# A new stored order and engine choice for the same pieces of an attention and spatial-gating kernel

## The chip, the core and the metric

The kernel runs on one core of a Trainium2 chip. TensorE multiplies matrices; VectorE, ScalarE and GpSimd do elementwise work; SyncE's queue issues the loads and stores. The metric is the time of one execution in microseconds of the device, as the median of several runs.

## What is computed

The inputs q, k and v have 8 batches, 8 heads, 576 positions and 64 channels. For each batch and head two attentions are added: one over means of four neighbouring positions (144 of them), repeated four times, and one where a position sees only those less than 4 away. The heads side by side are x (8, 576, 512), which goes through a gated block:

```python
    out_d = sm_attn(q_d, k_d, v_d)              # q_d, k_d, v_d: means over 4 positions
    out_up = np.repeat(out_d, factor, axis=2)
    mask = np.abs(pos[:, None] - pos[None, :]) < factor
    scores = np.where(mask, scale * np.matmul(q, k.transpose(0, 1, 3, 2)), -1000000000.0)
    ...
    return out_up + out_local
...
    h = x @ w_in                                # then gelu (tanh form)
    u, v = (h[..., :d_ff // 2], h[..., d_ff // 2:])
    v_n = (v - mu) / np.sqrt(var + 1e-06) * g_ln
    v_s = np.einsum('ts,bsd->btd', w_sg, v_n) + b_sg[None, :, None]
    return x + (u * v_s) @ w_out
```

## The kernel before, in words

The work is cut into 2105 small pieces ("tasks"), each with a name and one function that issues its instructions. A table in the source, `ORDER`, lists all names in the order in which they are issued; `/V`, `/A`, `/P` or `/S` behind a name chooses the engine (VectorE, ScalarE, GpSimd, SyncE's queue) where a piece can go to more than one. `place` walks the table once and deals out the buffers: 8 PSUM banks ("ps"), 10 wide buffers ("X") and 38 others ("R"). Each engine then works through its own pieces strictly in the table's order; a piece waits for what it reads and for its buffer to come free.

```python
    for word in ORDER.split():
        name, _, e = word.partition("/")
        t = named.pop(name)
        for k in t.takes:
            where[k] = free[k[0]].pop(0)
        ...
        order.append((t, e or next(iter(t.engines))))
```

Attention pieces carry the number g of a pair of heads, 0 to 31 (four pairs a batch). `lq`, `lk`, `lv`, `lw` load Q, K, V for the pooled part and V for the local part. `qs` and `ks` sum four neighbouring positions of Q and K (one reduction on VectorE, line 391, or two additions on GpSimd, lines 394 and 395). `Y` are the pooled scores (line 445), `S` the local ones (line 424, for the first four pairs with a mask product, line 417); from pair 4 on `YS` does both. `ma`, `mb` add the mask, `mx`, `my` take row maxima, `nx`, `ny` make the bias, `ea`, `eb`, `ec` the exponentials, `re`, `rc` the reciprocal of the sums, `np`, `nq` normalize (lines 506 and 509). `T`, `U`, `t` are the turns: transposes of the probabilities on TensorE (lines 512 and 521), which `pa`, `pb`, `pc`, `pe` copy out of PSUM. `D` multiplies the probabilities with V (lines 573 and 589), `vs` having summed V for it on GpSimd. `oe`, `od`, `xa`, `xb` put the two attentions together as x. `xh` and `xl` split x into a high and a low part (line 608 is the low part), `xc` copies a corner of it.

Y, S, YS and D are the 64-row products: each instruction uses 64 (or 48) rows and 64 columns of TensorE's array, four of them side by side. The turns and all products below use more than 64 rows; they are called 128-row here.

The gated block has per batch b: `v` (line 691, for batch 0 cut into `vk` and `v`), its gelu `vg`, statistics `vb`, root `vp`, normalization `vn` and split `vh`, `vl`; `u` (line 769) with gelu `ua`; `s` (line 769), the product over positions, with `sa` and gate `sm`; the split of the gated values `gh`, `gl`; and `o` (line 769) with the addition `oa` and the store `os`. The `w...` pieces load the weights and split them into two parts on ScalarE, VectorE and GpSimd. `wq0` to `wq4` are the loads of the spatial weights, `whq` and `wlq` their split.

TensorE issues one instruction after the other. No loop remains at run time: the table alone sets which product stands next to which.

Of the kernel before, what the change touches and what calls it, by code (L numbers as in the profile page):

```python
# [93 lines left out]
my3 ny4/V wuy2 eb3 wq4 lq5 qs5/V pc1/V mx4 lv1/S lk5 ny3/A t1 pe1/A wlq0/P np2/P T2 pa2/A ec3 re3/A wbz2 wuz3 rc3 wbz1
nq2/P U2 wty0 t2 wty2 pb2/A wuz1 wuz2 pc2/A pe2/V ks5/V ec4 lw1/S D1 oe1/V np3/P YS5 T3 od1 xa1 wqz3/A why0/A nx4/V
xb1 wly0/V vk3.0 wtz2 nq3/P U3 xh1/V xl1/P lv2 whq4/A lw2 wtz1 ea4 pa3/A vk2.0 ma5 eb4 lv3 my5 ny5/A re4/A mb5 wbz3
lk6 ks6/P pb3/A pc3/A wlq4/V rc4 np4/P D2 oe2/V od2 xa2 wr1 wqr1/A vk0.0 t3 lq6 ec5 wr2 why2/A wqr2/A wtz3 pe3/A mx5
nx5/A lw6 xb2 xh2/A vk3.1 whz1/A vk2.1 vk0.1 wbr1 lw3 whz2/A wz0 wqz0/A wuz0 wr0 vk4.0 T4 pa4/V xc1 wly2/P vk1.0 wbr2
vk4.1 vk1.1 D3 xl2/P xc2 vk4.2 vk2.2 vk1.2 whz3/A wbz0 oe3/A nq4/P U4 eb5 ea5 vk0.2 od3 xa3 xb3 vk3.2 wlz3/V wq1
whq1/A xh3/V t4 wtz0 lk12 xl3/V xc3 v0.1 pb4/A wlq3/V lq7 wlz1/V qs7/V qs6/V wlz2/P vg0.1 vb0.1 lv4 vs4 re5/V v0.2  # L100
v0.3 v0.0 pc4/A vg0.0 vb0.0 v0.4 lk9 whz0/A va0.4/A pe4/A vp0.0 u0.6 wq2 lq9 whq2/V vj0.4 vp0.1 rc5 nq5/P np5/P ua0.6
vg0.3 vg0.4 wur1 wr3 wqr3/A lw4 lq8 YS6 my6 ma6 u0.4 ua0.4 vn0.1 vh0.1/A vb0.4 ny6/A vg0.2 u0.7 vn0.0 vh0.0/A vp0.4
u0.5 ec6 mb6 vb0.2 wur3 vb0.3 mx6 wur0 wur2 ua0.5 U5 lk7 wlz0/P ks7/V nx6/A vn0.4 vh0.4/A wtr1 b lv5 vs5 ua0.7 lw11
lk8 ks8/V u0.2 ua0.2 wbr3 wlq2/V T5 pa5/A u0.0 ua0.0 vl0.1/V u0.1 vp0.2 vn0.2 vh0.2/A u0.3 ua0.3 vl0.0/V vp0.3 vn0.3
wlq1/V pb5/A ua0.1 vl0.2/V vh0.3/A vl0.3/P YS7 ma7 whr1/A wlr1/P ea6 D4 oe4/V qs9/V vl0.4/V my7 s0.1 sa0.1 sm0.1/P
pc5/V od4 xa4 s0.0 wtr3 eb6 sa0.0 mb7 qs8/V wtr2 re6/A rc6 t5 pe5/A ny7/A s0.3 sa0.3 ec7 mx7 whr3/A nx7/A YS8 my8 xb4
ma8 mb8 np6/P ks9/V wqr0/A nq6/P lk11 lv6 lq10 lw5 D5 oe5/A mx8 eb7 ny8/A ea7 T6 pa6/V sm0.0/V gh0.0/A s0.2 sa0.2
qs10/P od5 xa5 U6 s0.5 sm0.3/P sa0.5 lw8 vs6 wlr3/V sm0.2/P gh0.1/A re7/A s0.7 t6 s0.4 lv11 gl0.0/P xb5 pb6/V pc6/A
pe6/A wbr0 rc7 sm0.5/P lk14 xh5/A whr2/A lk10 sa0.7 np7/P lk15 ec8 lw7 lw14 lv7 sa0.4 nx8/V s0.6 sm0.4/P sa0.6 gh0.2/A
sm0.6/V gl0.2/V YS9 lq12 gl0.1/V D6 oe6/V ma9 mb9 mx9 nx9/V T7 sm0.7/P gh0.3/A lv12 lq11 gl0.3/P o0.6 oa0.6 ea8 eb8  # L110
re8/A od6 xa6 o0.4 oa0.4 my9 nq7/P U7 rc8 pa7/A pb7/V pc7/V nq8/V o0.7 ks10/V wtr0 ny9/A whr0/A t7 ec9 xb6 xh6/A pe7/V
o0.5 oa0.5 os0.2 YS10 oa0.7 os0.3 vs7 wlr0/P D7 oe7/A eb9 xh4/V ea9 re9/A ma10 mb10 mx10 od7 ks12/V wlr2/P t8 o0.3
np8/P T8 xa7 xb7 xh7/V o0.2 oa0.2 lq14 xl4/P xl5/V rc9 np9/V o0.0 lv9 lq13 xl6/P xc6 lv8 vs8 xc4 lq15 U8 pa8/A pb8/A
# [15 lines left out]
o1.2 oa1.2 re15/A pc14/A pe14/A vs13 D13 oe13/A od13 D14 my16 ny16/V u2.4 vb2.1 vp2.1 vp2.2 nx16/A eb16 rc15 np15/V
ec16 vn2.1 vb2.0 o1.3 ua2.4 o1.7 oa1.7 T15 o1.4 oa1.4 ea16 re16/A rc16 nq15/P o1.0 vp2.0 vn2.0 vh2.0/V vn2.2 xa13  # L130
oa1.0 vg2.4 vb2.4 pa15/A oe14/A u2.5 ua2.5 vh2.1/A vh2.2/A vp2.4 o1.5 oa1.5 vb2.3 u2.6 ua2.6 od14 o1.1 oa1.1 oa1.3
ks17/V t15 xb13 lv15 vn2.4 u2.0 vp2.3 vl2.1/P np16/P os1.0 lk18 xh12/A xa14 xl12/V vs15 U15 u2.7 T16 pa16/V xb14 u2.2
pb15/A pc15/A pe15/V vh2.4/V vl2.4/V u2.1 vl2.0/V ua2.0 ua2.2 ua2.1 YS17 ma17 vl2.2/V vn2.3 vh2.3/A mb17 ua2.7 xh13/V
my17 ny17/A ec17 lw15 D15 nq16/V oe15/A u2.3 od15 xa15 xb15 ks18/V vl2.3/P s2.1 sa2.1 sm2.1/P xh15/A xl15/V s2.7 s2.0
xl13/P YS18 ma18 xc15 ks20/P ua2.3 mb18 mx17 nx17/V mx18 nx18/A lk19 s2.2 ea17 sa2.0 xh14/V xl14/V U16 s2.3 sa2.3 t16
sm2.0/V gh2.0/A s2.5 sm2.3/V sa2.5 sa2.2 sm2.2/P lv20 eb17 re17/A pb16/A ea18 s2.4 sa2.4 gh2.1/A sm2.5/V rc17 pc16/A
s2.6 my18 ny18/A ec18 nq17/V eb18 np17/V re18/A sm2.4/P lw16 sa2.6 lv17 sa2.7 gl2.1/V u3.0 v3.1 xc13 U17 vs17 xc14
v3.2 vg3.2 vg3.1 sm2.6/V sm2.7/P gh2.3/A t17 rc18 pe16/V ks19/P xc12 v3.3 vg3.3 qs19/P gl2.0/P YS19 ua3.0 T17 pa17/V
# [850 lines left out]
```

## Time and profile before

| | |
|---|---|
| median of 3 runs | 582.2 us (581.97 to 583.54) |
| profiled execution | 582.29 us, its span 580.5 us |
| granted clock of TensorE over the span | 0.997 |
| instructions | 17400, of them 6992 matmuls and as many weight loads |
| moved | 52.64 MB read from HBM, 9.44 MB written |

The span runs from the first to the last instruction of the program; the execution's time is 1.8 us longer. Busy times are unions of an engine's instructions. TensorE's matmuls overlap each other, so what a matmul costs in a row of them is read from the distance of their starts, not from its own duration. "Idle before" is the time in which an engine did nothing just ahead of an instruction, and the arrow names what ended it; "issue" there means that nothing in the profile did.

### The profile page before, as it was taken

Reading aid. Unit: us, or ns where it says so; the run is one execution under the profiler, and the core shown is the slowest. Engines: PE = TensorE matmul, PEld = TensorE weight load, DVE = VectorE, ACT = ScalarE, POOL = GpSimd, SP = SyncE. Lnnn points to the kernel's source line nnn. Section 1 sums busy time; section 2 is a strip of 40 time slices with the busy share of each in tenths; the row PEclk is TensorE's granted clock in tenths of the full one; section 3 lists DMA queues with packets and bytes.
Section 4 is the critical chain, followed back from the end, with each engine's and each line's share of the span. In section 5 each row is a group of like instructions: output and inputs, shape, how many; then the busy total and the mean of one; then the engine's idle time right before and its main releaser. Section 6 shows DMA issues by size and latency. Waiting matters only on the chain.

```text
span 580.5 us, 17400 instructions
## 1 busy us (share of the span) xinstructions
PE 555.8 (96%) x6992; PEld 518.5 (89%) x6992; DVE 423.9 (73%) x926; ACT 350.5 (60%) x1237; POOL 312.1 (54%) x388
## 2 busy tenths in 40 slices
PE   5679999999999999999999999999998999999997
PEld 4568999889998899989999899989998899998997
DVE  5998899988988567848578778885967655653663
ACT  4988896759788864755438497728756357311200
POOL 4777857855378433574454646561475646541030
PEclk9999999999999999999999999999999999999999
DMA  8999256342132014161213606221255001010004
GB/s 312 350 284 336 83 151 191 124 142 69 57 106 76 23 44 129 53 201 49 70 38 103 213 25 190 78 84 65 76 164 140 22 1 57 1 43 1 21 0 184
DMA packets 30608, 63.20 MB, mean 109 GB/s; under 512 B 3520, under 2 KB 3776, under 8 KB 30528
## 3 DMA queue, kind: packets, MB, share of 16 engines
q1 hardware_dynamic: 30384, 61.79, 33.4%
...
q10 hardware_dynamic: 144, 0.30, 0.2%
q14 instruction: 25, 0.20, 0.1%
HBM read 52.64 MB, written 9.44 MB: 107 GB/s over the span
## 4 chain that ended last, share of the span: by engine, by line
PE 82%; DVE 9%; POOL 3%; issue 3%; ACT 2%; DMA 1%; DVEq 0%; ACTq 0%; POOLq 0%
PE ps L769 50%; PE ps L691 17%; PE ps L445 3%; PE ps L512 2%; PE ps L521 2%; PE ps L424 2%; PE ps L589 2%; PE ps L573 2%; POOL R L826 1%; POOL R L814 1%; DMA R<-in_qT_dram 1%; DVE R L221 1%; DVE R L596 1%; DVE X L432 1%; DVE R L740 1%
## 5 line engine op out<-in xcount | busy, mean ns | idle before, releaser
L769 PE MATMUL ps<-wsg_h,R 128*128 128x288 f32 x576 | 122.9, 300 | 1.2 <-DVE R L760 0.7
L769 PE MATMUL ps<-R,weight_r 128*128 128x288 f32 x768 | 110.0, 298 | 1.4 <-DVE R L826 0.6
L769 PE MATMUL ps<-X,weight_z 128*128 128x288 f32 x512 | 110.9, 299 | 0.0
L769 PEld LDWEIGHTS ps<-R,weight_r 128*128 128x128 f32 x768 | 103.4, 188 | 2.9 <-DVE R L826 0.9
L691 PE MATMUL ps<-weight_y,X 128*128 128x512 f32 x320 | 99.2, 402 | 0.3 <-DVE weight_y L326 0.2
L769 PEld LDWEIGHTS ps<-wsg_h,R 128*128 128x128 f32 x576 | 93.7, 188 | 2.0 <-DVE R L760 0.9
L484 ACT ACTIVATE X<-X,nb 128x64 f32<-128x64 f32 x280 | 93.5, 337 | 3.1 <-DVE nb L463 2.8
L769 PE MATMUL ps<-wsg_l,R 128*128 128x288 f32 x320 | 92.7, 295 | 0.0
L769 PEld LDWEIGHTS ps<-X,weight_z 128*128 128x128 f32 x512 | 84.5, 188 | 0.7
L769 PE MATMUL ps<-R,weight_z 128*128 128x288 f32 x256 | 75.4, 295 | 0.0
L691 PEld LDWEIGHTS ps<-weight_y,X 128*128 128x128 f32 x320 | 57.4, 188 | 12.0 <-DVE weight_y L326 0.5
L732 POOL TENSOR_TENSOR rs<-rs,nhalf 128x1 f32<-128x1 f32 (+1 forms) x40 | 23.3, 587 | 82.6 <-DVE rs L723 76.7
L769 PEld LDWEIGHTS ps<-wsg_l,R 128*128 128x128 f32 x320 | 60.3, 188 | 0.0
L807 DVE SCALAR_TENSOR_TENSOR vs<-ps,small_sb,b_sb 128x288 f32<-128x288 f32 x64 | 32.3, 512 | 29.1 <-PE ps L769 26.8
L484 ACT ACTIVATION_READ_ACCUMULATOR X<-X,nb 128x1 f32 x280 | 53.1, 189 | 0.0
L814 POOL TENSOR_TENSOR R<-R,vs 128x288 f32<-128x288 f32 x30 | 27.8, 929 | 44.5 <-DVE vs L807 43.3
L221 ACT COPY R<-ps 112x288 f32<-112x288 f32 (+4 forms) x75 | 27.8, 391 | 38.6 <-PE ps L521 16.2
L691 PE MATMUL ps<-weight_y,R 128*128 128x512 f32 x128 | 50.5, 394 | 0.6 <-issue 0.6
L788 ACT ACTIVATE R<-ps 128x288 f32<-128x288 f32 x64 | 24.8, 411 | 40.8 <-PE ps L769 34.9
L408 POOL TENSOR_TENSOR pairs<-R 112x256 f32<-112x256 f32 x56 | 46.7, 834 | 3.6 <-DMA R<-in_v_dram 3.5
L769 PEld LDWEIGHTS ps<-R,weight_z 128*128 128x128 f32 x256 | 48.2, 188 | 0.2
L721 DVE BATCH_NORM_STATS2 st<-R 128x6 f32<-128x512 f32 (+1 forms) x40 | 27.4, 686 | 27.5 <-ACT R L703 25.8
...
## 6 DMA issues: line engine op xcount, KB each, us to landing
...
```

The lines of the kernel that those rows point to most:

```text
L221: (nc.scalar.copy if e == "A" else ENG[e].tensor_copy)(**kw)
L408: ENG[e].tensor_tensor(out=pairs, in0=v[:, 0:2], in1=v[:, 2:4], op=ALU.add)
L424: nc.tensor.matmul(out=sp[i][os, c * KB:(c + 1) * KB], lhsT=q[hs, t * QB:t * QB + KB], rhs=k[hs, t * QB:t * QB + KB], start=not early, sto ...
L445: nc.tensor.matmul(out=st["sdv"][n][os, cs], lhsT=qd2[par][hs, i * QC:i * QC + HD], rhs=st["kd"][hs, ks], start=True, stop=True)
L484: nc.scalar.activation(out=st["ms"][:, t, :], in_=src, func=AF.Exp, bias=st["nb"][:, t:t + 1], scale=scale, accum_out=sums[par][:, t:t + 1])
L691: nc.tensor.matmul(out=acc, lhsT=r32(l), rhs=r32(weights[f"y{k}"][:, 0, w]), start=(i == 0 and ks[0] == 0), stop=(i == len(ops) - 1 and ks ...
L721: nc.vector.bn_stats(out=st6[0:n], in_=v[0:n])
L732: nc.gpsimd.tensor_tensor(out=rs[0:n], in0=rs[0:n], in1=nhalf[0:n], op=ALU.pow)
L769: nc.tensor.matmul(out=acc[:, 0:HALF], lhsT=r32(l), rhs=r32(r), start=(first and n == 0), stop=(last and n == len(ops) - 1))
L788: nc.scalar.activation(out=us[i // 2][:, half(i)], in_=at["ps", "m", b, "u", i][:, 0:HALF], func=AF.Gelu_apprx_tanh)
L807: nc.vector.scalar_tensor_tensor(out=vsb[i], in0=at["ps", "m", b, "s", i][:, 0:HALF], scalar=g_sb[:, i // 2:i // 2 + 1], in1=b_sb[:, half( ...
L814: ENG[e].tensor_tensor(out=u[:, half(i)], in0=u[:, half(i)], in1=vsb[i], op=ALU.mult)
```

## The change

Only `ORDER` differs: the same 2105 names stand in it in another order, some with another engine. No piece, no size and no buffer count is changed. Of the pieces with a choice of engine, VectorE has 14 fewer, GpSimd 15 more and ScalarE one fewer; among them GpSimd takes 24 normalizations `np` where it had 19 and 24 of the `vl` where it had 18, ScalarE takes 22 of the `xh` where it had 13 and 20 of the `pe` where it had 13, and gives up 9 of 19 `oe` and 9 of 26 `re`. On the queues of loads the first K comes by ScalarE's queue and the first Q by SyncE's, the other way round than before.

The table's rows tell a reader little; one of each:

```diff
-nq0/P U0 lq4 mx2 nx2/A wly3/V pa0/V pb0/V pc0/V lv0/S t0 eb1 pe0/A whq0/V wty1 why1/V wly1/P lk3 ks3/V lq3 S3 re1/A
...
+wqy3/V nq0/V T0 why0/V wly0/P t0 U0 pa0/V pb0/V pc0/V pe0/V Y2 my2 wqz1/V nx2/A eb1 re1/V why1/V rc1 np1/P nq1/P lk4
```

What that does to an engine shows in the engine's own rows (line, operation, what it writes and reads, size). The first place is GpSimd's queue in the opening. Names: `half`, `qd` and `kd` are the sums of Q and K, `pd` and X (line 506) the normalized probabilities, `weight_y` the weights of v, line 319 and line 326 two steps of their split, line 608 the low part of x. Before, from the second step of weight y1 on:

```order
L326 TENSOR_TENSOR weight_y1_332<-R5_198,weight_y1_332 128x512
L394 TENSOR_TENSOR half_380<-R9_303 128x288
L395 TENSOR_TENSOR qd0_75<-half_380 128x144
L506 TENSOR_TENSOR X1_241<-X1_241,rc1_95 128x640
L608 TENSOR_TENSOR R18_463<-R17_457,X4_461 128x576
L394 TENSOR_TENSOR half_475<-R16_385 128x288
L395 TENSOR_TENSOR kd0_83<-half_475 128x144
L509 TENSOR_TENSOR pd1_88<-pd1_88,rc1_95 128x9x48
```

and now, from the same step on:

```order
L326 TENSOR_TENSOR weight_y1_339<-R3_147,weight_y1_339 128x512
L394 TENSOR_TENSOR half_449<-R13_356 128x288
L395 TENSOR_TENSOR qd0_75<-half_449 128x144
L394 TENSOR_TENSOR half_463<-R19_438 128x288
L395 TENSOR_TENSOR kd1_84<-half_463 128x144
L319 TENSOR_TENSOR R14_359<-R14_359,weight_z1_235 128x512
L608 TENSOR_TENSOR R27_600<-R18_434,X5_503 128x576
```

The sum `kd0` that YS4 reads stood behind the low part of x (L608); it has moved to VectorE, `kd1` here is pair 3's, and the low part of x stands behind the sums and a weight's step.

The second place is TensorE at pair 19. `X` read in line 512 and `pd` in line 521 are its probabilities; lines 769 are products of s and u, line 424 is the end of YS21. Before, its turn T, then a product of u, and later U and t apart from it:

```order
L769 MATMUL ps_4852<-wsg_h,R_4699 128x288
L769 MATMUL ps_4852<-wsg_l,R_4699 128x288
L512 MATMUL ps_4868<-small_sb,X_4314 128x122 x4
L769 MATMUL ps_4877<-X_3707,weight_z_902 128x288
L769 MATMUL ps_4877<-R_3711,weight_z_902 128x288
```

and now T, t and U in one row behind the 64-row products of YS21:

```order
L424 MATMUL ps_4943<-R_3956,R_3688 64x64 x2
L424 MATMUL ps_4944<-R_3956,R_3688 64x64 x2
L512 MATMUL ps_4965<-small_sb,X_4266 128x122 x4
L521 MATMUL ps_4970<-small_sb,pd_88 112x112 x2
L512 MATMUL ps_4981<-small_sb,X_4266 128x122
L521 MATMUL ps_4981<-small_sb,pd_88 112x112 x3
L769 MATMUL ps_4989<-wsg_h,R_4489 128x288
```

The turn left its place between two 128-row products and came to stand between 64-row products and a 128-row one; t and U joined it.

Around the piece YS4 TensorE's table read S3, Y2, D0, T1, YS4, U1, Y3, and reads Y2, D0, T1, S3, U1, YS4, t1, Y3 now. Behind the opening, groups of three 64-row pieces stood at YS24 D21 D22, YS27 D24 D25, YS29 D26 D27 and YS31 D28 D29; they stand at YS17 D14 D15, YS22 D18 D19, YS23 D20 D21 and D26 D27 YS30.

More of the change, by code (lines that the diff above doesn't have):

```diff
@@ L94 @@
[L94 to L113, printed above, removed]
@@ L129 @@
[L129 to L138, printed above, removed]
@@ L169 @@
-u5.1 u5.3 ua5.3 vh5.4/A ua5.1 vl5.3/V oa4.4 oa4.5 qs28/P YS28 my28 xh24/V ny28/A T26 pa26/A vl5.4/V s5.2 U26 pb26/V
-ma28 mb28 mx28 pc26/A s5.1 sa5.1 nx28/V eb28 lv26 T27 pa27/A s5.4 xl24/P t26 ec28 lw27 lk29 lw26 lv27 ks29/P qs29/V
-pe26/V xl25/P os4.2 vs26 vs27 s5.0 sa5.0 sm5.0/V s5.3 t27 sa5.2 sm5.2/P sm5.1/V lk31 gh5.0/V sa5.4 sa5.3 s5.6 U27
-pb27/A pc27/V sm5.3/V gh5.1/A ea28 s5.5 sm5.4/V sa5.6 pe27/V sa5.5 sm5.5/V gh5.2/A s5.7 sa5.7 sm5.7/V YS29 ma29 my29
-mb29 ny29/V lw29 D26 oe26/A re28/V rc28 gl5.0/P mx29 sm5.6/P gh5.3/A ec29 od26 D27 oe27/A od27 xa27 nx29/A eb29
@@ new lines @@
+lw14 T15 pa15/A U15 vh2.3/A ks17/V vb2.4 vp2.4 oa1.6 vh2.0/A o1.7 oa1.7 lw16 pb15/A pc15/A my16 ny16/A o1.2 vb2.2 mx16
+nx16/V U14 t14 t15 o1.3 ec16 pe15/A o1.5 oa1.5 eb16 o1.1 oa1.1 u2.1 vp2.2 vn2.2 vh2.2/V vl2.2/P vl2.3/P oa1.2 oa1.3
+pb14/V os1.2 vl2.0/P lq21 lw15 os1.3 vh2.1/A vl2.1/P ea16 vn2.4 u2.3 ua2.3 u2.0 ua2.0 qs17/V os1.0 vh2.4/V pc14/V YS17
+ma17 qs19/P pe14/A re16/A D14 mb17 mx17 oe14/A od14 vl2.4/V xa14 xb14 rc16 nq16/V D15 ks19/V oe15/V np16/V s2.1 nx17/A
+eb17 od15 xa15 xb15 xh15/A xl15/P ua2.1 lv17 lk18 my17 ks18/V s2.0 sa2.0 sm2.0/V sa2.1 lq18 qs18/P ny17/V sm2.1/V u2.6
@@ new lines @@
+ua3.2 ua3.3 nx20/V ea20 lv19 ua3.7 lw20 lw26 os2.2 od17 nq19/V xa17 np19/P s3.2 sm3.0/P sm3.1/P sa3.3 ks21/P qs22/V
+gh3.0/V eb20 xb17 xh17/A vs19 ec20 sa3.2 sm3.2/P xh16/V sm3.3/P s3.4 sa3.4 sm3.4/P gh3.1/A gl3.0/P s3.6 sa3.6 sm3.6/P
+s3.5 YS21 T19 t19 re20/V my21 sa3.5 ma21 ny21/A rc20 U19 ec21 s3.7 pa19/V pb19/V pc19/A pe19/A ks22/V YS22 os2.3 D18
+oe18/A sm3.5/V gl3.1/P np20/P gh3.2/V gl3.2/P sa3.7 sm3.7/P ma22 mb22 lw19 D19 mb21 nq20/V T20 mx21 pa20/V od18 oe19/V
+od19 xa18 xa19 xb19 xb18 xl16/V mx22 gh3.3/A gl3.3/P nx21/A xl17/V o3.3 o3.6 o3.4 oa3.4 U20 ea21 xh19/A my22 o3.5 eb21
@@ new lines @@
+mx23 vp4.4 D20 oe20/V ec23 D21 od20 oe21/V od21 xa20 U22 pb22/V xb20 xa21 xb21 u4.7 vs22 nx23/A ea23 eb23 u4.1 ua4.1
+os3.0 lq26 u4.3 t22 lw23 os3.3 ks25/P vn4.4 re23/V ua4.7 vp4.3 vn4.3 vh4.4/V os2.0 lq29 lw24 lk27 u4.5 ua4.5 u4.2
+ua4.2 qs25/V ua4.3 pc22/A rc23 nq23/V vh4.3/V vl4.3/P YS24 my24 ny24/A pe22/A lv23 t23 lw31 lv24 vl4.4/V lq27 s4.1
+sa4.1 ec24 ma24 mb24 mx24 nx24/A eb24 ea24 xh21/V s4.0 xh20/V sa4.0 YS25 ma25 mb25 mx25 np23/P nx25/V D22 oe22/A od22
+my25 ny25/V lk26 eb25 T23 xa22 s4.6 xl21/V lq31 xb22 xh22/A qs26/P pa23/V ks26/V s4.3 sm4.1/P sa4.3 ea25 re24/V
@@ new lines @@
+s5.0 oa4.0 pc26/A ua5.3 o4.1 sa5.0 np27/P ea28 sm5.0/V re28/A gh5.0/A s5.2 sa5.2 lk29 oa4.1 o4.4 o4.5 oa4.4 os4.0 lq30
+ks29/P s5.3 sa5.3 rc28 lk30 lw28 pe26/V oa4.3 qs29/P YS29 my29 gl5.0/P U27 np28/P T27 pa27/A pb27/V pc27/V ks30/P ma29
+mb29 oa4.5 mx29 nx29/A xh24/A sm5.3/V s5.5 s5.4 sa5.5 sm5.2/V gh5.1/A sa5.4 sm5.5/V nq28/V ny29/V sm5.4/V eb29 gl5.1/V
+gh5.2/A qs30/V gl5.2/V os4.2 s5.7 sa5.7 sm5.7/P lv31 lv29 s5.6 sa5.6 sm5.6/P t27 pe27/V ec29 T28 pa28/V U28 pb28/V
+pc28/A D26 oe26/V od26 ea29 D27 oe27/A gh5.3/V gl5.3/P xl24/P xa26 xb26 YS30 my30 ma30 t28 ny30/A ec30 od27 xh26/V
@@ L193 @@
+s7.5 sa7.5 o6.7 sm7.5/P gh7.2/A s7.6 s7.7 sa7.7 sm7.7/V sa7.6 sm7.6/V oa6.6 oa6.7 os6.3 os4.3 os6.0 os6.2 gl7.2/P ok3
+ok2 ok1 ok0 gh7.3/A gl7.3/V o7.2 oa7.2 o7.3 oa7.3 os7.1 o7.0 oa7.0 o7.1 oa7.1 o7.4 oa7.4 o7.6 oa7.6 os7.3.0 os6.1 o7.5
+oa7.5 os7.2 os7.0 o7.7 oa7.7 os7.3.1
 """
```

148 lines of the change are left out of this document (80 added, 68 removed).

## The prediction

> **What bounds the kernel now.** I read first the page's busy line, then the windows of the whole run, then the waits of TensorE, then the timeline at the places that these name. The busy line:
>
> ```profile
> span 580.5 us, 17400 instructions
> PE 555.8 (96%) x6992; PEld 518.5 (89%) x6992; DVE 423.9 (73%) x926; ACT 350.5 (60%) x1237; POOL 312.1 (54%) x388
> ```
>
> TensorE is the bound: 24.7 us of the span are not matmul. The profiled execution took 582.29 us beside a median of 582.2, so its rows stand for the runs as they are; 1.8 us lie outside the span. Where the idle time lies is told by the windows (stretch and its length; busy time and instructions of TensorE's matmuls, its weight loads, VectorE, ScalarE and GpSimd; granted clock; share and GB/s of DMA):
>
> ```profile
> 0.00:14.50 14.50, 8.43 (x124) 5.87 (x124) 7.52 (x18) 6.54 (x28) 6.23 (x16) 1.00 0.89 312
> 14.50:29.00 14.50, 9.07 (x252) 7.50 (x254) 13.57 (x36) 14.19 (x79) 11.22 (x14) 0.95 1.05 350
> 29.00:43.50 14.50, 10.89 (x249) 8.88 (x246) 13.26 (x31) 11.65 (x52) 10.88 (x10) 0.93 0.91 283
> 43.50:58.00 14.50, 13.88 (x252) 11.70 (x245) 12.33 (x23) 12.01 (x49) 10.89 (x12) 1.00 1.03 337
> 58.00:77.00 19.00, 19.00 (x180) 17.88 (x178) 17.39 (x40) 17.18 (x38) 14.41 (x19) 1.00 0.20 64
> 77.00:154.00 77.00, 74.33 (x1131) 68.62 (x1132) 69.99 (x150) 58.81 (x216) 49.44 (x59) 1.00 0.46 138
> 154.00:515.00 361.00, 358.06 (x4404) 338.57 (x4405) 258.38 (x570) 222.13 (x767) 198.90 (x248) 1.00 0.27 82
> 515.00:580.00 65.00, 62.13 (x428) 59.45 (x426) 31.42 (x67) 7.99 (x17) 10.13 (x14) 1.00 0.14 51
> ```
>
> In the first 58 us TensorE idles 15.7 us (58 less 8.43, 9.07, 10.89 and 13.88). From 58 to 515 it idles 5.6 us in all (0, 2.67 and 2.94). The rest is the end, where the last products, the last addition and the last store follow each other. A new order of the same pieces can gain in the opening or in the price of the matmuls themselves; the middle has almost nothing to give and much to lose. The longest waits of TensorE (who waited for whom: total, times, longest) say what the opening waits for:
>
> ```profile
> PE ps L445 <- POOL qd L395: 6.1, 1, 6.1
> PE ps L445 <- POOL kd L395: 3.6, 1, 3.6
> PE ps L589 <- issue: 2.2, 1, 2.2
> ```
>
> The 6.1 is the wait for the first loads and sums. It stays: the sums of K and Q only trade engines and queues, and one of the two is still made by GpSimd's pair of instructions.
>
> **The change, part by part: turns beside 64-row products.** I counted groups in the two stored orders. Groups of 64-row pieces (Y, S, YS, D that follow each other): 36 before, 36 after. So the number of changes from 128-row to 64-row work and back is the same, and the second half of the change's description is true only if turns are not counted as 128-row work. What moved are the turns: 25 groups of 64-row pieces are followed by a turn where 15 were, and turns that follow another turn rise from 8 to 37. The timeline prices this. First a YS, its turn and the products behind; then a YS with products right behind it; then a turn between products:
>
> ```profile
> 421.08 0.29 PE L769 MATMUL ps<-X,weight_z 128*128 128x288 f32 x1
> 421.30 0.56 PE L445 MATMUL ps<-kd,qd 64*64 64x144 f32 x10
> ...
> 422.49 0.64 PE L512 MATMUL ps<-small_sb,X 122*128 122x122 f32 x4
> 422.89 0.51 PE L769 MATMUL ps<-wsg_h,R 128*128 128x288 f32 x2
> ```
>
> ```profile
> 458.44 0.56 PE L445 MATMUL ps<-kd,qd 64*64 64x144 f32 x10
> ...
> 459.62 0.40 PE L769 MATMUL ps<-X,weight_z 128*128 128x288 f32 x1
> ```
>
> ```profile
> 461.19 0.29 PE L769 MATMUL ps<-X,weight_z 128*128 128x288 f32 x1
> 461.32 0.58 PE L512 MATMUL ps<-small_sb,X 122*128 122x122 f32 x4
> 461.67 0.38 PE L769 MATMUL ps<-X,weight_z 128*128 128x288 f32 x1
> ```
>
> Starts tell the price. Going into a 64-row group takes 0.22 us (421.08 to 421.30) where a product follows a product in 0.13 (461.19 to 461.32). A YS runs 1.19 us until a turn can start (421.30 to 422.49) and 1.18 us until a product can (458.44 to 459.62): the turn pays the way out just as a product does. And the four instructions of a turn take 0.40 us behind a 64-row group, 0.35 between products. So a turn moved behind 64-row work is dearer by 0.05 us, and ten more such places cost 10 x 0.05 = **+0.5 us**. Joined turns I cost at nothing: each instruction still takes its 0.1 us step. Bounds: 0 (no turn dearer) and +0.9 (each at the 0.09 us that the way in costs).
>
> **The opening.** Here most of the 15.7 us lie. The longest wait behind the first is that of YS4:
>
> ```profile
> 27.75 0.88 PE L445 MATMUL ps<-kd,qd 64*64 64x144 f32 x10 [3.57 <-POOL kd L395]
> ...
> 29.86 0.46 PE L512 MATMUL ps<-small_sb,X 122*128 122x122 f32 x1
> ...
> 39.28 0.53 PE L445 MATMUL ps<-kd,qd 64*64 64x144 f32 x11 [1.93 <-DVE kd L391]
> ...
> 40.44 0.64 PE L512 MATMUL ps<-small_sb,X 122*128 122x122 f32 x4
> ```
>
> ```profile
> 25.15 1.41 POOL L608 TENSOR_TENSOR R<-R,X 128x576 fp32r<-128x576 f32 x1 [1.66 <-DVE X L221]
> 26.52 0.67 POOL L394 TENSOR_TENSOR half<-R 128x288 f32<-128x288 f32 x1
> 27.27 0.43 POOL L395 TENSOR_TENSOR kd<-half 128x144 f32<-128x144 f32 x1
> ```
>
> The sum of K for YS4 stood on GpSimd behind the low part of x (L608), which itself waited 1.66 us for VectorE. In the new order that sum is VectorE's, the low part of x comes behind the sums of Q and K on GpSimd, and S3 stands between T1 and YS4. What is late next is S3's K: by the order of the queue about 7.1 MB are asked for up to it, which at the 312 to 350 GB/s of the first two windows is 20 to 23 us and a landing; D0 and T1 fill TensorE till about then. I expect YS4 near 26 us instead of 27.75.
>
> There is a second price in those rows. YS4 took 2.11 us (27.75 to 29.86) and YS5 1.16 (39.28 to 40.44). The granted clock says why:
>
> ```profile
> 27.60:31.10 3.50, 3.35 (x68) 2.94 (x69) 2.44 (x7) 2.99 (x18) 3.50 (x5) 0.51 1.01 239
> 31.10:39.20 8.10, 4.75 (x132) 4.03 (x124) 8.03 (x18) 6.31 (x23) 6.02 (x6) 1.00 0.85 243
> ```
>
> Right behind the wait of 3.57 us the clock is halved for 3.5 us; matmuls worth about 1.7 us of full speed are stretched by as much. If no wait of that length is left, 1.7 us go with it. The Trainium skill, page "TensorE: Matmul & The Clock Gate", Part 1, says that the clock drops to half after an idle window of about 3.4 us and that a free-running window decides it. This trace agrees (3.57 us, then 0.51). By that rule the sum below would be 1.7 us higher if S3 waited for its K longer than one window, and as it stands if each wait left is shorter. What such a wait costs as a rival (2, below) is priced from the rows above alone.
>
> Then the queues. Ahead of D1 the new order has fewer pieces on the two engines that are full between 14.5 and 43.5 us (VectorE 13.57 and 13.26 of 14.5, ScalarE 14.19 and 11.65): on VectorE 18 pieces are gone and 11 new, on ScalarE 11 gone and 4 new. Of VectorE's, the sums (five gone, three new) and a normalization of 640 columns are the large ones:
>
> ```profile
> L391 DVE TENSOR_REDUCE kd<-R 128x144 f32<-128x576 f32 x19 | 14.1, 740 | 3.4 <-DMA R<-in_kT_dram 3.4
> L506 DVE TENSOR_TENSOR X<-X,rc 128x640 f32<-128x640 f32 x13 | 13.1, 1006 | 0.3
> ```
>
> Net two sums (1.5 us) and that normalization (1.0) are 2.5 us; with a weight's shift, a maximum, a copy of x and casts of spatial weights gone and two short normalizations come I estimate 4 to 5 us less VectorE work ahead of D1. TensorE's own work ahead of it is less by a T, a U and a t only. So TensorE may be 4 to 5 us ahead when the first v products start.
>
> It will not keep that. Ahead of YS7 (77 us before) ScalarE has more to do than it had: three copies of x and three of the spatial weights and two weight scalings come to it, and two activations of u and an exponential of three go behind.
>
> ```profile
> L221 ACT CAST X<-R 128x576 fp32r<-128x576 f32 x13 | 8.8, 675 | 8.3 <-DVE R L596 8.3
> L221 ACT CAST wsg_h<-R 128x576 fp32r<-128x576 f32 x2 | 1.4, 686 | 0.0
> L303 ACT ACTIVATE weight_r<-weight_r 128x512 f32<-128x512 f32 x4 | 2.8, 688 | 0.0
> L788 ACT ACTIVATE R<-ps 128x288 f32<-128x288 f32 x64 | 24.8, 411 | 40.8 <-PE ps L769 34.9 <-POOL R L760 2.5 <-POOL vd L409 1.4
> L492 ACT ACTIVATE pd<-ps,nbd 128x144 f32<-128x144 f32 x96 | 35.4, 379 | 6.4 <-PE ps L521 3.8 <-DVE nbd L475 2.1
> ```
>
> 8 x 0.68 = 5.4 us in, 2 x 0.41 + 3 x 0.38 = 2.0 us out, and the other pieces, a scaling among those that leave, take back some 1.2 more: +2.2 us, in a stretch where ScalarE is already at 17.18 of 19.00. TensorE idles 0.00 there now; 2 us of its lead go into waiting for ScalarE. Net for the opening: **-2.6 us**, with the bounds -6 (the lead of 4 to 5 is kept and the half clock's rest comes to it) and +1 (no lead, and half of ScalarE's 2.2 us lands on TensorE).
>
> **The middle.** Of its 5.6 us, 2.2 are a wait that nothing releases, inside a row of three 64-row pieces (YS29, D26, D27):
>
> ```profile
> 442.04 0.58 PE L589 MATMUL ps<-R,X 64*64 64x58 f32 x22
> ...
> 444.83 0.45 PE L589 MATMUL ps<-R,X 64*64 64x58 f32 x15 [2.21 <-issue]
> ```
>
> Such rows of three stand four times in the old order and four times in the new, at other places; one of the four stalls now. I take half of it as gone, **-1.1 us** (bounds -2.2 and +6.6, all four stalling). Against that the new order leaves less room: places where TensorE's own work between a piece and the one that hangs on it is under 1 us more than the chain between are 68 where 43 were (my count from both orders with durations of the trace). Before, 43 such places and 3.4 us of real waits; 25 more at 0.08 us each would be 2 us, but most lie in the opening, already counted: **+0.6 us** (0 to +2). The engines themselves do not bind: VectorE is at 72% from 154 to 515 us (258.38 of 361). The end I cost at nothing: the same pieces follow the last product of s in both, and the last products are the bound there.
>
> **Sum:** 582.3 + 0.5 - 2.6 - 1.1 + 0.6 = **579.7 us**, 0.4% under the median.
>
> **Rivals.** (1) ScalarE takes back all of the lead between 58 and 77 us. For it: 90% busy there, 2.2 us more to do. Against: copies of weights can wait, and u has PSUM room. Then the opening gives 0: 582.3, no change. (2) The half clock returns, as S3 waits over 3.4 us for its load. For it: its K stands behind three more weights. Against: TensorE has Y2, D0 and T1 in front. +1.7: 581.4, no change. (3) Slower: the rows of three 64-row pieces stall as at 442 us. Place: YS17 D14 D15, YS22 D18 D19, YS23 D20 D21, D26 D27 YS30; price 2.2 us each. It decides from three on: 582.3 + 0.5 - 2.6 + 0.6 + 3 x 2.2 - 2.2 = 585.2; two give 583.0. For it: the one in the trace; against: three of four ran through.
>
> **How the numbers follow.** A measurement here tells a difference from none from about 0.3%, 1.75 us: faster is under 580.45, slower over 583.95. Forecast 0.52 (its own range 575.8 to 581; 0.50 lies under 580.45), rival 1 0.20, rival 2 0.08, rival 3 0.20. So faster 0.50, same 0.30, slower 0.20. The range 575.8 to 584.8 takes in the two middle rivals and most of the third, and at its low end nearly the whole bound of the opening.
>
> **What would show it.** Right: the windows to 58 us show 12 to 13 us of TensorE idle instead of 15.7 and a clock of 1.00 from 24 to 36 us; YS4 starts near 26 us; TensorE idles about 1 to 2 us from 58 to 77; turns behind 64-row groups take 0.40 us. Wrong: idle over 8 us between 77 and 515, waits on issue inside rows of three, or a long wait on ScalarE before YS7.

## Result, and the profile after

| | before | changed |
|---|---|---|
| median | 582.87 us of 4 runs (581.97 to 584.16) | 576.45 us of 4 runs (574.64 to 578.38) |
| profiled execution | 582.29 us, span 580.5 us | 574.64 us, span 572.9 us |
| granted clock over the span | 0.997 | 1.000 |

The ratio is 0.9889, interval 0.9845 to 0.9932: the new order is 1.1% faster. The busy line of the changed kernel's page:

```profile
span 572.9 us, 17455 instructions
PE 552.4 (96%) x6992; PEld 517.2 (90%) x6992; DVE 407.7 (71%) x912; ACT 356.6 (62%) x1236; POOL 320.8 (56%) x403
```

The windows of the changed kernel at the same places as before, the last one cut at its own end (stretch and length; busy time and count of TensorE's matmuls, weight loads, VectorE, ScalarE, GpSimd; clock; share and GB/s of DMA):

```profile
0.00:14.50 14.50, 8.31 (x123) 5.64 (x124) 6.31 (x16) 5.94 (x23) 5.91 (x16) 1.00 0.87 312
14.50:29.00 14.50, 10.06 (x241) 7.65 (x244) 14.21 (x36) 13.54 (x72) 10.76 (x12) 1.00 1.03 298
29.00:43.50 14.50, 12.70 (x353) 10.89 (x347) 14.08 (x31) 13.85 (x66) 13.93 (x14) 1.00 1.04 308
43.50:58.00 14.50, 13.44 (x181) 11.13 (x174) 11.84 (x26) 12.87 (x46) 11.64 (x14) 1.00 1.03 353
58.00:77.00 19.00, 19.00 (x281) 18.09 (x281) 18.02 (x43) 16.29 (x37) 12.66 (x15) 1.00 0.20 59
77.00:154.00 77.00, 76.54 (x1115) 72.30 (x1114) 64.60 (x150) 63.07 (x252) 62.75 (x81) 1.00 0.46 145
154.00:515.00 361.00, 357.90 (x4356) 339.17 (x4355) 251.91 (x562) 221.39 (x727) 190.99 (x242) 1.00 0.26 80
515.00:572.90 57.90, 54.43 (x379) 52.33 (x377) 26.70 (x56) 9.63 (x19) 12.15 (x15) 1.00 0.17 62
```

To 58 us TensorE idles 13.5 us (15.7 before) at a full clock; from 58 to 77 still nothing; from 77 to 154 only 0.46 (2.67 before); from 154 to 515 3.1 (2.94 before). In 77 to 154 the loads are evened out: VectorE falls from 69.99 to 64.60, GpSimd rises from 49.44 to 62.75.

Idle time understates a stall, because a matmul's modelled end reaches into the gap behind it (the stall at 304 us below has 1.77 us of idle time and 2.0 from start to start). So I also worked out **lost time**: each TensorE piece's median distance to the next start, by kind, is taken as its price, and the lost time at a place is the start of the piece there less the prices of all pieces ahead of it. The sum of these prices is called TensorE's work below; "lost by 60" is the lost time where 60 us of work are done. It compares orders at equal work done. The prices are those of the full clock, so a half clock counts as lost time too. One profiled execution each; all columns behind the clock in us:

| kernel | clock | lost by 60 | 60 to 160 | 160 to the end | all |
|---|---|---|---|---|---|
| before | 0.997 | 16.2 | 6.4 | 5.5 | 28.1 |
| changed | 1.000 | 13.6 | 1.9 | 4.9 | 20.4 |
| changed, again | 0.996 | 17.1 | 1.9 | 4.5 | 23.5 |
| open_only | 0.994 | 15.5 | 5.8 | 4.8 | 26.1 |
| first_part | 0.997 | 16.0 | 2.2 | 6.8 | 25.0 |
| rest_only | 0.994 | 16.5 | 6.0 | 4.7 | 27.2 |
| middle_only | 0.985 | 15.6 | 8.6 | 6.8 | 31.0 |
| two_waits | 0.988 | 15.6 | 11.9 | 7.0 | 34.5 |
| mended | 0.991 | 17.1 | 5.9 | 4.3 | 27.3 |
| turns_out | 1.000 | 13.6 | 3.0 | 8.2 | 24.8 |
| split3 | 0.994 | 14.9 | 1.9 | 4.0 | 20.8 |
| first_split | 0.997 | 13.4 | 2.1 | 4.2 | 19.7 |
| order_alone | 0.963 | 23.5 | 28.3 | 48.3 | 100.1 |
| engines_alone | 0.953 | 33.7 | 27.9 | 44.5 | 106.1 |

Of the 7.7 us between before and changed, 2.6 lie in the opening, **4.5 between 60 and 160 us of TensorE's work** (by 60 + 16.2 and 160 + 22.6, 76 to 183 us of the execution before), 0.6 behind. TensorE's waits in 77 to 165 us before (for whom: total, times, longest; from 165 to 185 us neither trace shows one):

```profile
PE ps L769 <- DVE R L760: 0.7, 1, 0.7
PE ps L769 <- DVE R L826: 0.6, 1, 0.6
PE ps L445 <- ACT R L788: 0.6, 1, 0.6
PE ps L769 <- DVE R L596: 0.5, 1, 0.5
PE ps L769 <- POOL R L826: 0.2, 1, 0.2
```

and all that the changed kernel has there:

```profile
PE ps L769 <- ACT pd L492: 0.5, 1, 0.5
```

By lost time the waits before are larger than their rows: s0.1 (L760, the low part of v) 1.0, o0.6 (L826, the low part of the gated values) 1.5, o0.2 0.7, D10 0.9.

### The profile page after: what moved, and what is told of

The parts are those of the page before. It is cut to its first block, busy times and chain, and to the rows that moved or that the text cites. A ratio compares the mean times of both kernels' runs of the same rounds, so it can differ in the third digit from the quotient of the medians.

```text
span 572.9 us, 17455 instructions
## 1 busy us (share of the span) xinstructions
PE 552.4 (96%) x6992; PEld 517.2 (90%) x6992; DVE 407.7 (71%) x912; ACT 356.6 (62%) x1236; POOL 320.8 (56%) x403
## 5 line engine op out<-in xcount | busy, mean ns | idle before, releaser
L769 PE MATMUL ps<-wsg_h,R 128*128 128x288 f32 x576 | 121.4, 298 | 0.1
L769 PE MATMUL ps<-X,weight_z 128*128 128x288 f32 x512 | 109.0, 297 | 0.5 <-ACT pd L492 0.5
L769 PE MATMUL ps<-R,weight_r 128*128 128x288 f32 x768 | 107.4, 296 | 0.0
L691 PE MATMUL ps<-weight_y,X 128*128 128x512 f32 x320 | 97.8, 399 | 0.0
L814 POOL TENSOR_TENSOR R<-R,vs 128x288 f32<-128x288 f32 x34 | 28.6, 848 | 54.7 <-DVE vs L807 30.4
L221 ACT COPY R<-ps 112x192 f32<-112x192 f32 (+4 forms) x74 | 28.1, 395 | 45.8 <-PE ps L512 14.4
L221 ACT CAST R<-R 128x576 fp32r<-128x576 f32 (+2 forms) x46 | 29.5, 648 | 36.0 <-DVE R L814 15.1
L843 DVE TENSOR_TENSOR R<-ps,R 128x288 f32<-128x288 f32 x64 | 27.8, 450 | 30.2 <-PE ps L769 30.2
L760 POOL TENSOR_TENSOR R<-R,R 128x512 fp32r<-128x512 f32 (+1 forms) x24 | 32.2, 1349 | 30.0 <-DVE R L221 14.9
```

Source lines behind the costliest of these rows:

```text
L221: (nc.scalar.copy if e == "A" else ENG[e].tensor_copy)(**kw)
L691: nc.tensor.matmul(out=acc, lhsT=r32(l), rhs=r32(weights[f"y{k}"][:, 0, w]), start=(i == 0 and ks[0] == 0), stop=(i == len(ops) - 1 and ks ...
L760: ENG[e].tensor_tensor(out=r32(dst), in0=vact[s][0][0:n], in1=vh[0:n, 0:DM], op=ALU.subtract)
L769: nc.tensor.matmul(out=acc[:, 0:HALF], lhsT=r32(l), rhs=r32(r), start=(first and n == 0), stop=(last and n == len(ops) - 1))
L814: ENG[e].tensor_tensor(out=u[:, half(i)], in0=u[:, half(i)], in1=vsb[i], op=ALU.mult)
L843: nc.vector.tensor_tensor(out=x[:, half(i)], in0=at["ps", "m", b, "o", i][:, 0:HALF], in1=x[:, half(i)], op=ALU.add)
```

## Experiments

Each was timed in five rounds beside the kernel before on the same chip. All edit `ORDER` alone.

**Where the gain lies: open_only, first_part, rest_only, middle_only.** Words up to one piece from one order, the rest from the other.

```diff
 open_only:   new order up to s0.1 | old behind
-mx7 s0.1 sa0.1 ea6 sm0.1/P lk11 my7 eb6 ...
+mx7 lk12 lk9 ec6 lw11 wbr3 whr1/A wlr1/P ea6 qs9/V my7 s0.1 sa0.1 sm0.1/P s0.0 ...
 first_part:  new order up to YS14 | old behind
-s1.2 YS14 ma14 mb14 mx14 xh8/A xh9/A ...
+sm1.0/V ea13 YS14 sa1.2 ma14 D11 my14 oe11/V T12 ...
 rest_only:   old order up to YS14 | new behind
-s1.2 YS14 sa1.2 ma14 D11 my14 oe11/V ...
+s1.2 lw13 lk16 lq19 YS14 ma14 mb14 mx14 xl9/P ...
```

Expected of open_only:

> The new order up to the first product s of batch 0 (about 77 us), then all remaining pieces in the old order with the old engines. Theory 1 (the gain is waits that went, part in the opening and part between 77 and 165 us): TensorE is 2.6 us ahead at s0.1, as in the changed kernel, and the old waits behind it come back, so 2 to 3.5 us faster than before, 579.5 to 581. Rival (turns beside 64-row products save the changes of mode): 3 of 25 such places lie here, so under 1 us. Rival (the opening's lead is taken back by queues later): no difference.

Expected of first_part:

> The new order up to YS14 (about 155 us of the changed kernel), the rest in the old order and engines. Theory 1: the whole lead of 6 to 7 us that the changed kernel has at that place is kept to the end, 575.5 to 577. Rival (turns beside 64-row products): 11 of the 25 places lie here, so half of the gain at most, 579.5 or more.

Expected of rest_only:

> The old order up to YS14, the new one from there. Theory 1: the old opening and the old waits up to 165 us stay, so hardly a gain: 0 to 1.5 us faster, 581 to 583. Rival (turns beside 64-row products): 14 of the 25 places are in this part, so about half of the gain, 579 to 580.

Measured: open_only 579.56 us, ratio 0.9944 (0.9925 to 0.9963); first_part 576.25, 0.9886 (0.9858 to 0.9914); rest_only 582.16, 0.9993 (0.9977 to 1.0008). All three as expected. The whole gain lies ahead of YS14 (159 us in the changed kernel). Behind it stand 14 of the 25 turns that follow 64-row groups, and the rows of three; in rest_only, which has them without the rest, no gain shows. open_only alone gives half.

The stretch from s0.1 to YS14 alone, with the old opening (`vl0.4` ahead of `oe4`, `lw11` held back for want of a wide buffer):

```diff
-ea6 D4 oe4/V qs9/V vl0.4/V my7 s0.1 sa0.1 sm0.1/P pc5/V od4 xa4 s0.0 wtr3 ...
+ea6 D4 vl0.4/V oe4/V qs9/V my7 wtr2 whr2/A od4 xa4 wqr0/A xb4 wlr2/V pc5/A t5 ... s0.1 sa0.1 sm0.1/P lk11 eb6 ...
```

> The old order up to s0.1 (with vl0.4 ahead of oe4, and lw11 held back to its new place), the new one from there to YS14, the old one behind: about the new order between 77 and 155 us without the new opening. Theory (the losses between 60 and 160 us of TensorE's own work fall from 6.4 to about 2 through the order and engines of this stretch alone, whatever the opening did): 3 to 4.4 us faster than before, near 579; up to 1.5 us of it may go at the seam, where old and new pieces of VectorE and ScalarE meet. Rival (the stretch gains only because the new opening hands TensorE and the engines over in another state): losses of 5 us or more there, 0 to 1.5 us faster, 581 to 582.6.

Measured: 585.15 us, 1.0032 (1.0014 to 1.0051), slower than either theory allowed. Its own waits, of TensorE:

```profile
PE ps L769 <- DVE R L596: 3.4, 1, 3.4
PE ps L445 <- ACT weight_z L303: 1.6, 1, 1.6
```

At the seam pieces that the new order had done in the opening (od4, xa4, xb4, four steps of weights) came in front of s0.1 at once: 6.2 us were lost between 60 and 80. Part of that is the clock: behind the wait of 3.4 us the granted clock was 0.50 from 81.5 to 88.3 us. From 80 to 160 it lost 2.4 (5.3 before, 1.8 changed). That does not prove the stretch's own worth: open_only, with the old order there, also lost only 2.7 from 80 to 160, after 3.1 lost at its seam. Whoever makes TensorE wait gives the other engines time, and less is lost behind. What is shown is narrower: the five profiled executions of orders with both the new opening and the new stretch as they are lost 1.9 to 2.2 between 60 and 160, whether 13.4 or 17.1 were lost before; each part alone lost 5.8 to 8.6. (turns_out, below, has both, but with the turns moved: 3.0.)

**Order and engines apart: order_alone, engines_alone.** The new order with each piece's old engine, and the old order with each piece's new one (the first loads of Q and K excepted). The engine differs for 324 of the 718 words that name one: the few pieces by which the engines' counts differ are what is left of many exchanges.

```diff
 order_alone (against the changed kernel)
-xa7 rc9 xb7 xh7/V np8/P T8 lk12 lv13 nq8/P o0.2 t8 xl4/P xl6/P xc6 oa0.2 xl7/P ...
+xa7 rc9 xb7 xh7/V np8/P T8 lk12 lv13 nq8/V o0.2 t8 xl4/P xl6/P xc6 oa0.2 xl7/V ...
 engines_alone (against the kernel before)
-T7 sm0.7/P gh0.3/A lv12 lq11 gl0.3/P o0.6 ...
+T7 sm0.7/V gh0.3/A lv12 lq11 gl0.3/V o0.6 ...
```

> The new order with the old choice of engine for every piece (the first Q and K on the queues of the new one). If the order does it alone: within 1 us of the changed kernel, 575.5 to 577.5. If order and engines belong together, since VectorE is at over 90 percent up to 150 us: waits on VectorE and GpSimd come back in the opening and at o0.6, 578 to 584.

> The old order with the new choice of engine (the first Q and K as before). If the engines do it alone: 576 to 578. If the two belong together: no gain or a loss, 581 to 588, with new waits of TensorE on GpSimd, which gets 15 more pieces in places that were not made for them.

Measured: order_alone 653.84 us, 1.1230 (1.1202 to 1.1258); engines_alone 659.83, 1.1322 (1.1292 to 1.1352). Both expectations missed by far. TensorE's largest waits behind the first in order_alone:

```profile
PE ps L512 <- DVE X L506: 6.2, 4, 2.6
PE ps L445 <- DVE qd L391: 5.1, 2, 3.1
PE ps L521 <- DVE pd L509: 4.1, 1, 4.1
PE ps L691 <- POOL X L221: 4.0, 1, 4.0
```

and in engines_alone:

```profile
PE ps L521 <- ACT R L221: 5.7, 1, 5.7
PE ps L769 <- POOL R L826: 4.3, 2, 3.5
PE ps L769 <- ACT pd L492: 3.8, 2, 2.8
```

No single wait carries it; the lost time grows all along (28 us of it between 60 and 160, over 44 behind). The half clock has a share: 0.963 over 652.6 us is up to 24 us of the lost time, and 0.953 over 658.5 us up to 31; before, 0.997 is 1.7. My reading is that a table's row names a place in four queues at once: a piece on another engine, at the same place, stands behind pieces that are themselves waiting, and everything behind it on that engine waits too. With 322 pieces exchanged at once, what is shown is that neither half works without the other, so the gain can't be split into one of the order and one of the engines.

**Two waits by hand: two_waits.** In the kernel before, the low part of v earlier, and the last gate and split of batch 0 on VectorE.

```diff
-ea6 D4 oe4/V qs9/V vl0.4/V my7 s0.1
+ea6 D4 vl0.4/V oe4/V qs9/V my7 s0.1
-T7 sm0.7/P gh0.3/A lv12 lq11 gl0.3/P o0.6
+T7 sm0.7/V gh0.3/A lv12 lq11 gl0.3/V o0.6
```

> The kernel before with three small edits at the two longest waits between 77 and 110 us: vl0.4 is put ahead of oe4 and qs9 on VectorE (s0.1 waited for it, and oe4 itself waits for D4), and sm0.7 and gl0.3 go from GpSimd to VectorE (o0.6 waited for them). Theory 1 (those waits are the end of queues and are worth their length): the extra 0.97 us at s0.1 and most of the 1.46 us at o0.6 go, 1.5 to 2.4 us faster, 580.5 to 581.5, and the lead stays to the end. Rival (the next wait takes it back): no difference at the end, though the two waits are gone from the trace.

Measured: 588.77 us, 1.0097 (1.0070 to 1.0125): 5.9 us slower, where 1.5 to 2.4 faster was expected. The first edit did its work (17.3 lost by 80 before, 16.2 here). The second edit, of the gate and the split, made the wait that it was to remove longer. ScalarE's and TensorE's timeline:

```profile
103.68 0.79 PE L769 MATMUL ps<-R,weight_r 128*128 128x288 f32 x4 [2.38 <-DVE R L826]
106.15 0.67 ACT L221 CAST R<-R 128x576 fp32r<-128x576 f32 x1 [5.97 <-DVE R L814]
106.87 2.36 PE L769 MATMUL ps<-R,weight_r 128*128 128x288 f32 x7 [2.41 <-ACT R L221]
```

The gate sm0.7 (L814) now stood in VectorE's queue behind oe6, which waits for D6, and the four pieces ma9 to nx9; ScalarE's gh0.3 waited 5.97 us for it, and o0.6 for gh0.3. VectorE was busy 69.99 of 77 us in this stretch before: it was the wrong engine to give more to. Behind the two waits of 2.4 us the clock was 0.50 from 106.1 to 113.0 us, so up to 3.4 us of the loss there is the clock: a wait can cost more than its length. These two words are among the edits of engines_alone.

**Three losses by hand, no engine changed: mended.**

```diff
-ea6 D4 oe4/V qs9/V vl0.4/V my7 s0.1
+ea6 D4 vl0.4/V oe4/V qs9/V my7 s0.1
-lw10 D10 oe10/A YS13 ... xc10 u1.5
+u1.5 lw10 D10 oe10/A YS13 ... xc10
-D26 ... od26 D27 oe27/A od27 xa27 nx29/A ... o5.6
+D26 ... od26 nx29/A ... o5.6 D27 oe27/A od27 xa27
```

> The kernel before with three edits and no engine changed: vl0.4 stands ahead of oe4 and qs9 (VectorE), u1.5 ahead of D10 (TensorE), and D27 behind o5.6, so that the row YS29 D26 D27 is cut. Theory (a wait of TensorE behind the opening is lost for good and worth its length where its repair puts no new piece in front of another engine's waiting one): the losses at s0.1 (1.0 us), D10 (0.9) and in the row of three (2.0 to 2.4) go, together 3.5 to 4.3 us faster, near 579; the lead of TensorE over the kernel before is 1.0 at 80 us of its own work, about 1.9 at 160 and about 4 at the end. Rival (TensorE only arrives earlier at the next wait, which another engine's own chain sets): the lead of 1.0 is gone at o0.6 and the one of D10 at YS13; only the row of three is left, 2.0 to 2.4 us faster, near 580.7.

Measured: 580.83 us, 0.9967 (0.9951 to 0.9982), 1.8 us faster: near the rival's 2.0 to 2.4, and 2 us short of the theory's. Piece by piece (lost at that piece, against before): s0.1 -0.94, but over 60 to 80 only -0.6 is kept; D10 -1.05, but YS13 +0.54 and T11 +0.56 right behind; D27 -2.45, but o5.6 +1.07. The two new waits:

```profile
156.80 0.61 PE L512 MATMUL ps<-small_sb,X 122*128 122x122 f32 x4 [0.28 <-DVE R L596]
444.51 0.40 PE L769 MATMUL ps<-R,weight_r 128*128 128x288 f32 x1 [0.69 <-POOL R L826]
```

Where TensorE comes sooner, it meets the next thing that another engine has not done yet. A wait removed alone is worth what the next chain lets through, here between nothing and two thirds of its length.

**The turns: turns_out.** The changed kernel with 21 of its 25 turns behind 64-row groups moved behind the product that follows, with their copies and what hangs on those.

```diff
-wlq0/P D4 lq7 vb0.1 vp0.1 T5 pa5/A vp0.0 oe4/A ... vn0.2 u0.0 xa4
+wlq0/P D4 lq7 vb0.1 vp0.1 vp0.0 oe4/A ... vn0.2 u0.0 T5 pa5/A xa4
...
```

> The changed kernel with 21 of the 25 rows of turns that follow 64-row products moved behind the product that follows them (with the pieces that hang on them), so that each stands between two 128-row products. By the price of the prediction (0.05 us for a turn behind 64-row work): 21 x 0.05 = 1.05 us faster than the changed kernel, or nothing where later copies make waits. By the rival (turns beside 64-row products save changes of mode, 0.09 us in and 0.13 us out): 2 to 4.6 us slower than the changed kernel.

Measured: 581.03 us, 0.9972 (0.9949 to 0.9995), 4.6 us slower than the changed kernel's median (3.8 slower than its second one, below). The rival gave this number, but its reason does not show in the trace: a D in front of a product takes 1.14 us from start to start, as a D in front of a turn did. The trace lost 4.4 us more than the changed kernel's first one, and more than half of it (1.6 and 1.4) stands at two waits, at o0.6 and at YS22:

```profile
PE ps L769 <- DVE R L826: 1.2, 1, 1.2
PE ps L445 <- ACT pd L492: 1.2, 1, 1.2
```

At YS22 the moved turns are the cause: the exponentials of pair 21 waited 2.5 us on ScalarE for pair 19's turns (line 521), which stand later now, and YS22 waited for these exponentials. At o0.6 they are not shown to be: VectorE's last gate and split took 1.72 and 1.89 us in place of 0.46 and 0.75, and why is open. So what the run shows is narrower than a price of turns: an early turn lets other engines start the work that hangs on it early.

**The rows of three: split3, first_split.** In the changed kernel D19 behind o3.3 and D21 behind u4.7; in first_part D27 behind o5.6.

```diff
 split3
-lw19 D19 mb21 ... o3.3 o3.6
+lw19 mb21 ... o3.3 D19 oe19/V od19 xa19 xb19 o3.6
-D20 oe20/V ec23 D21 ... u4.7
+D20 oe20/V ec23 ... u4.7 D21 oe21/V od21 xa21 xb21
```

> The changed kernel with the two rows of three 64-row pieces that stall on issue taken apart: D19 stands behind o3.3 and D21 behind u4.7. If the stall comes of so many short instructions in a row: both stalls (1.98 and 1.07 us over the usual step) go, two more changes of mode cost 0.4, so 2 to 2.6 us faster than the changed kernel. If it hangs on where in the program the instructions are fetched: the stalls stay or move, and it is 0 to 0.5 us slower.

> The new order up to YS14 and the old one behind it, as in first_part, with D27 behind o5.6. Theory (the row YS29 D26 D27 stalls because one instruction fetch comes too late for some 300 short matmuls, and a 128-row product between them gives it time): 2.0 to 2.4 us faster than first_part, near 574, faster than both kernels; no wait on issue near 440 us. Rival (the stall goes to the next 64-row group, or the later D27 makes a wait for its copies): as first_part, 576 to 576.5.

> The changed kernel as it is, as a base on the same chip as the two others. 575 to 578, ratio 0.985 to 0.992. Theory and rival say the same of it; it tells whether first_split and split3 are faster than it by more than the runs differ.

Measured: split3 575.02 us, 0.9869 (0.9837 to 0.9900); first_split 575.73, 0.9876 (0.9852 to 0.9900); the changed kernel, on first_split's chip, 577.25, 0.9906 (0.9874 to 0.9938). The stalls on issue inside the rows are gone in both. What split3 has instead around the first of them:

```profile
PE ps L769 <- POOL R L826: 0.7, 1, 0.7
```

Its o3.3 waits for its gated values, as o5.6 did in mended and does in first_split: the stall had covered that wait. In the traces split3 lost 4.0 behind 160 (4.9 changed; 2 to 2.6 less was expected), first_split 4.2 (6.8 first_part). The 2.6 between the last two look like the theory's size and are not: in first_part's trace the clock was 0.50 from 441.0 to 444.4 us, right behind its stall, and in first_split's it was not. At the row itself the stall's 2.4 us went and 1.2 came back at o5.6. By the medians split3 is 1.4 us under the changed kernel (on another chip) and first_split 1.5 under it on the same chip; the intervals overlap, so neither is shown to be faster than the changed kernel, while both are faster than the kernel before. The medians of first_split and first_part, from different chips, differ by 0.5, near the rival's forecast and not the theory's 574.

## Why the prediction was right, and where it was wrong

Forecast 579.7, range 575.8 to 584.8, 0.5 on faster; measured 576.45 (577.25 the second time): on the right side and inside the range. The profiled 574.64 lies outside. A gain of 2.6 us was forecast and 6.4 measured (582.87 to 576.45). The range held it by luck: its low end was the bound of the opening, and the larger part of the gain came from the middle, of which the prediction said that it had almost nothing to give.

**Turns, +0.5: the price right, the term incomplete.** Behind 64-row work a turn of four takes 0.39 us, between products 0.34 (starts in the changed kernel's timeline):

```profile
384.60 0.86 PE L424 MATMUL ps<-R,R 64*64 64x64 f32 x40
385.40 0.64 PE L512 MATMUL ps<-small_sb,X 122*128 122x122 f32 x4
385.79 0.71 PE L691 MATMUL ps<-weight_y,X 128*128 128x512 f32 x2
...
```

```profile
259.06 0.58 PE L512 MATMUL ps<-small_sb,X 122*128 122x122 f32 x4
259.40 0.38 PE L769 MATMUL ps<-X,weight_z 128*128 128x288 f32 x1
```

But the joined turns, costed at nothing, are not free: in the changed kernel a T in front of another turn takes 0.42 us from start to start and in front of a product, between products, 0.34; a t takes 0.19 and 0.13. At 0.07 us each the 29 more joined turns are an estimated +2.0. Against them, 39 fewer turns follow a product, and that step is dearer in some places and not in others (s in front of a U takes 1.95 us before, in front of a product 1.87; in the changed kernel 1.87 and 1.86). What the turns cost TensorE in sum is therefore open. turns_out shows that their place matters through the engines that wait for them, which the term did not have.

**Opening, -2.6: the size met in one pair of profiles, by other steps; luck in part.** 16.2 lost by 60 before, 13.6 after, but 17.1 in the second profile (next point). The seven traces with the new opening lost 14.9 by 60 on average (13.4 to 17.1), the five with the old one 16.2 (15.6 to 17.1): 1.3 us less, with ranges that overlap. The idle time to 58 us is 13.5, where 12 to 13 was forecast, and the clock is 1.00 throughout, as forecast. But YS4 starts at 28.56, not near 26. Start, length and work of TensorE, in brackets what it waited:

```profile
23.53 0.64 PE L512 MATMUL ps<-small_sb,X 122*128 122x122 f32 x4 [0.45 <-POOL X L506]
24.85 1.31 PE L417 MATMUL ps<-small_sb 128*128 128x256 f32 x4 [0.69 <-DVE R L311]
...
26.96 0.32 PE L512 MATMUL ps<-small_sb,X 122*128 122x122 f32 x1
...
28.56 0.56 PE L445 MATMUL ps<-kd,qd 64*64 64x144 f32 x10 [0.99 <-DVE stats L454]
```

S3 (L417) and U1 stand in front of it now, and it waits for VectorE's maxima (L454) and no longer for its sum. The lead was 4.3 us at 24 us of TensorE's work and 2.6 at 60, so 1.7 of it went back, by 36 us of work already. The step that was to take it back failed: ScalarE was to get 2.2 us more to do from 58 to 77 us and TensorE to idle 1 to 2 us there. ScalarE is busy 16.29 us there (17.18 before), and TensorE idles 0.00. The longest wait behind the first is 2.0 us (total, times, longest):

```profile
PE ps L445 <- POOL kd L395: 6.7, 2, 6.2
PE ps L589 <- issue: 2.6, 2, 1.8
PE ps L512 <- POOL X L506: 2.4, 2, 2.0
```

**Rival 2, the half clock, did come, in four of the seven traces with the new opening.** The second profile of the changed kernel, windows of its opening, and the turn T0 there:

```profile
16.00:18.00 2.00, 0.47 (x25) 0.34 (x17) 2.00 (x7) 2.00 (x11) 1.85 (x3) 1.00 1.10 236
18.00:20.00 2.00, 1.74 (x10) 1.41 (x10) 1.62 (x4) 2.00 (x14) 0.85 (x1) 0.72 1.00 298
20.00:22.00 2.00, 2.00 (x32) 1.83 (x34) 1.38 (x5) 1.13 (x7) 0.44 (x1) 0.50 1.04 378
22.00:24.00 2.00, 2.00 (x95) 2.00 (x88) 1.97 (x7) 2.00 (x10) 0.76 (x1) 0.92 1.09 278
```

```profile
17.98 0.64 PE L512 MATMUL ps<-small_sb,X 122*128 122x122 f32 x4 [1.53 <-POOL X L506]
```

and the same turn in the first profile, where the clock stayed at 1.00:

```profile
17.98 0.64 PE L512 MATMUL ps<-small_sb,X 122*128 122x122 f32 x4 [2.00 <-POOL X L506]
```

From 18.9 us on the clock is halved for 3.4 us, 1.7 us of clock, behind a wait of 1.5 us; in the first profile a wait of 2.0 at the same place left it whole. The rival named S3's load as the place and a wait over 3.4 us as the condition: both wrong, the price right. The rule of the Trainium skill, page "TensorE: Matmul & The Clock Gate", Part 1, that a free-running window decides fits the difference between two executions of one order; its figure of an idle window of about 3.4 us ahead of the drop does not fit this row, where the wait is 1.5 us.

The traces show how two executions of one order can differ here: every stretch at one clock between the first change and the end of the products lasts a multiple of 3.41 us (3.41, 6.83, 17.07 and so on), so the changes lie on a grid, which stands elsewhere in each execution. In the second profile the whole wait lies in one piece of the grid (15.48 to 18.89), and the next piece is at half; in the first a boundary at 17.30 cuts the wait in two. Of the other five traces with the new opening, open_only, split3 and first_split (1.8 of its 2.0 us) are like the second and turns_out is like the first. first_part is an exception: 1.8 us of its wait lie in one piece, and the clock stays whole. The second profile also idles 2.8 us from 43.5 to 58 (1.1 in the first). The clock over the span was 0.985 to 1.000 in the changed kernel's ten runs, and 0.988 to 0.997 in the 16 runs of before beside the last six of them. So the half clock belongs to no one order; it is a part of the spread of the runs, and the gain of the stretch behind is the same with and without it (1.9 lost in both profiles).

**Issue, -1.1: wrong, +0.6.** The stall at 442 us went, and two others came, in YS22 D18 D19 and YS23 D20 D21:

```profile
304.16 0.57 PE L589 MATMUL ps<-R,X 64*64 64x58 f32 x24 [1.77 <-issue]
...
341.55 0.57 PE L589 MATMUL ps<-R,X 64*64 64x58 f32 x23 [0.86 <-issue]
```

By starts 2.0 and 1.1 were lost, 3.0 together, against 2.4 before. "Half of it as gone" had no reason but the count of one in four; it was two in four. Rival 3 needed three. A wait on issue inside a row of three was one of the signs of being wrong that the prediction had named.

**Middle, +0.6: the step that failed.** It is the term of the sum that was mis-sized: measured -4.5 between 60 and 160. It rested on the count of places with under 1 us of room (68 where 43 were), and on the idle rows, by which "the middle has almost nothing to give". Both misled. The idle time of 77 to 154 us, 2.67, stood for nearly all of the 6.4 lost by starts. And the room of a place, worked out from durations alone, says nothing of what stands ahead of the chain in the other engines' queues: in two_waits and mended this is what set the wait. The new order has more tight places and fewer waits. What made the waits go is shown only as far as this: both parts of the order are needed, with their engines. That the load moved from VectorE (91% busy in this stretch before, 84% after) to GpSimd (64% to 81%) is in the windows and fits, but no run isolates it: it stays open.

**The end, 0,** as forecast: from the start of the last product to the end of the span it is 5.1 us before and 5.2 now. Rival 1 (ScalarE takes all of the lead back from 58 to 77) did not come; idle 0.00 there.
